# Attention scores over 64-key half-blocks in 32x64 tiles of TensorE, 76 score steps in place of 96

## The chip, the cores and the metric

The kernel runs on one core of a Trainium2 chip. The metric is the device time of one execution in microseconds. Five engines work side by side and meet through semaphores: TensorE (PE in the profile; its weight loads are PEld), VectorE (DVE), ScalarE (ACT), GpSimd (POOL) and SyncE (SP), which here only issues transfers. Each engine works off its own instructions in the order in which the program issues them.

## The reference

The input is normalized, and the sum of three terms is returned: the input itself, a sliding-window attention of 32 heads of 16 with a window of 256 keys, and a gated bilinear layer.

```python
xn = layernorm(x)                                  # x: 1 x 2048 x 512, bf16
# A: H = 32, Dh = 16, W = 256
q, k, v = split(xn @ wqkv)
scores = einsum("bhqd,bhkd->bhqk", q, k) * Dh ** -0.5
mask = (i - j >= 0) & (i - j < W)                  # query i, key j
o = einsum("bhqk,bhkd->bhqd", softmax(where(mask, scores, -1e9)), v)
a = o.reshape(B, S, D) @ wo
# B: F = 1792
b = ((xn @ w_gate) * (xn @ w_up)) @ w_down
return x + a + b
```

## The kernel before

The 2048 rows are cut into four chunks T of 512, and a chunk into four blocks of 128. All weights stay on the chip. The work falls into two kinds.

**Attention** goes by score steps. A group c has eight heads: four at even positions (parity 0) and four at odd positions (parity 1). The four heads e of one c and parity lie in four groups of 32 rows of TensorE, so their four matmuls run side by side, each in a 32x128 tile, and write four banks of the tile `S` (`scores`, L244). Keys stand on the partitions of the result and queries along the columns. A query block needs three key blocks: its own, masked to a triangle, the one before it, unmasked, and the one two before it, masked to the opposite triangle. `GROUPS` (L16) lays the twelve pairs of blocks of one chunk, c and parity into three strips of 512 columns: three steps, each with one exponential of 128x2048 on ScalarE (L252) and two or three triangles cut by GpSimd (L257, L261). With 4 chunks, 4 c, 2 parities and 3 strips there are 96 steps. `S` has one buffer, so a step's scores wait for the exponential of the step before.

Two steps (`LAG`) after the third strip of a c and parity, `values` (L277) multiplies the strips with V: four tiles of 128 rows x 32 columns side by side, one for each head, into the single accumulator `accb`. V has a column of ones, so the same matmul gives the sum of the softmax. VectorE transposes the accumulator (L284), takes the reciprocal (L286) and divides (L297); after parity 1 it transposes the result (L300).

**Fillers** are everything else: projections of the next chunk (`proj_v` L184, `proj_qk` L196), gate and up (L310, L321), down, the output projection and its store (L338, L344, L362), normalization of the next chunk. They are full 128x128 matmuls of 512 columns, four to a tile of gate or up. Their results go to a pool of three PSUM banks (`ps_m`): VectorE empties gate (L315), up (L325), K and Q (L201, L202, L207); ScalarE empties V (L188).

The order is written out in `run`: the loop goes over the score steps; after each it issues values that are due and then as many fillers as `upto` allows, which shares the planned TensorE time over the steps (here weighted by a step's blocks). The fillers' order is fixed in `fillers`: for each chunk down and output projection of the chunk before, then gate and up, then the projections of the next chunk. `before` and `after` keep a filler ahead of the step that needs it, or behind the one whose result it needs. Since engines work in order, what is issued on VectorE or ScalarE ahead of an eviction also runs ahead of it.

The start is separate: `setup` issues the first four blocks of x and the V weights alternately from SyncE and ScalarE (L62, L64), and `first_chunk` normalizes block by block, with the statistics of the fourth block on ScalarE and GpSimd (`norm_stats_act`, L133), and the first block's normalization and transposes in halves.

Of the kernel before, what the change touches and what calls it, by code (L numbers as in the profile page):

```python
# [11 lines left out]
ALU = mybir.AluOpType  # L12
# [3 lines left out]
GROUPS = (  # L16
    ((-2, 0, 0, 0), (0, 0, 2, 128)),
    ((-1, 0, 1, 0), (2, 2, 3, 256)),
    ((1, 1, 3, 0), (3, 3, 3, 384)),
)  # L20


class Kernel:
    def __init__(self, ctx, tc, x, wqkv, wo, wg, wu, wd, out):
        self.tc, self.nc = tc, tc.nc
        _, S, D = x.shape
        self.S, self.D, self.F = S, D, wg.shape[1]
        assert D == 512 and S % 512 == 0 and self.F % 256 == 0
        self.NT, self.NCH, self.NF = S // 128, S // 512, self.F // 128
        self.x_d, self.out_d = x.flatten_outer_dims(), out.flatten_outer_dims()  # L30
        self.w_d = dict(qkv=wqkv, o=wo, g=wg, u=wu, d=wd)

        def pool(name, bufs, **kw):
            return ctx.enter_context(tc.tile_pool(name=name, bufs=bufs, **kw))

        self.const = pool("const", 1)
        self.chunk2 = pool("chunk2", 2)
        self.chunk3 = pool("chunk3", 3)
        self.ppool = pool("ppool", 6)
        self.work = pool("work", 3)  # L40
        self.xpool = pool("xpool", 4)
        self.small = pool("small", 4)
        self.ypool = pool("ypool", 5)
        self.ps_s = pool("ps_s", 1, space=bass.MemoryType.PSUM)
        self.ps_a = pool("ps_a", 1, space=bass.MemoryType.PSUM)
        self.ps_m = pool("ps_m", 3, space=bass.MemoryType.PSUM)


    def setup(self):
# [11 lines left out]
        for b in range(4):  # L61
            (nc.scalar if b % 2 else nc.sync).dma_start(out=self.x[:, b, :], in_=xv[:, b, :])  # L62
        for k in (0, 2):
            (nc.scalar if k else nc.sync).dma_start(out=self.Wqkv[:, k:k + 2, 1024:1536], in_=wq[:, k:k + 2, 1024:1536])  # L64
        for lo in (512, 0):
# [32 lines left out]
        nc.gpsimd.memset(self.mhalf[:], -0.5)  # L98
        self.xnT, self.Q, self.hT, self.O, self.OT = {}, {}, {}, {}, {}
        self.K, self.Ko, self.V = {}, {}, {}  # L100
        self.strips, self.at = {}, {}

    def new_chunk(self, T):
# [5 lines left out]
        self.nc.gpsimd.memset(self.V[T][:, :, :, 16:18], 1.0)  # L109

# [22 lines left out]
    def norm_stats_act(self, t):  # L133

        nc = self.nc
        sums = self.small.tile([128, 2], F32, tag="sums", name="sums")
        for j, func in enumerate((ACT.Copy, ACT.Square)):
            junk = self.xpool.tile([128, 512], BF16, tag="xn", name="junk")
            nc.scalar.activation(out=junk[:], in_=self.x[:, t, :], func=func, accum_out=sums[:, j:j + 1])
        mv = self.small.tile([128, 1, 2], F32, tag="mv", name="mv")  # L140
        mean, sq = mv[:, 0, 0:1], self.small.tile([128, 2], F32, tag="sq", name="sq")
        nc.gpsimd.tensor_scalar(out=mean, in0=sums[:, 0:1], scalar1=1.0 / 512, scalar2=None, op0=ALU.mult)
        nc.gpsimd.tensor_scalar(out=sq[:, 0:1], in0=sums[:, 1:2], scalar1=1.0 / 512, scalar2=None, op0=ALU.mult)
        nc.gpsimd.tensor_tensor(out=sq[:, 1:2], in0=mean, in1=mean, op=ALU.mult)
        nc.gpsimd.tensor_tensor(out=mv[:, 0, 1:2], in0=sq[:, 0:1], in1=sq[:, 1:2], op=ALU.subtract)
        self.stats[t] = [mv, 0, None]

    def norm_apply(self, t):
# [3 lines left out]
        for c0, c1 in ((0, 256), (256, 512)) if t == 0 else ((0, 512),):  # L152
            nc.vector.tensor_scalar(out=xn[:, c0:c1], in0=self.x[:, t, c0:c1], scalar1=mv[:, j, 0:1],  # L153
                                    scalar2=rs[:, j:j + 1], op0=ALU.subtract, op1=ALU.mult)
        self.xns[t] = xn

    def norm_transpose(self, t, by_dma):
# [9 lines left out]
        for k0, k1 in ((0, 2), (2, 4)) if t == 0 else ((0, 4),):  # L167
            ps = self.ps_m.tile([128, 4, 128], BF16, tag="M", name="xTp")
            for k in range(k0, k1):
                nc.tensor.transpose(ps[:, k, :], xn[:, 128 * k:128 * k + 128], self.ident[:])  # L170
            nc.scalar.activation(out=self.xnT[T][:, b, k0:k1, :], in_=ps[:, k0:k1, :], func=ACT.Copy)
# [37 lines left out]
    def first_chunk(self):  # L209

        self.new_chunk(0)
        for b in (0, 1):
            self.norm_stats(b, 1)
            self.norm_scale(b, 1)
        self.norm_stats_act(3)
        self.norm_apply(0)
        self.norm_stats(2, 1)
        self.norm_scale(2, 1)
        self.norm_scale(3, 1)
        for b in (1, 2, 3):  # L220
            self.norm_apply(b)
        self.norm_transpose(0, False)
        for b in range(4):
            if b < 3:
                self.norm_transpose(b + 1, False)
            self.proj_v(b)
        self.proj_qk(0, 0, 1)
# [4 lines left out]
    def parts(self, T, i):  # L232
        return [p for p in GROUPS[i] if 4 * T + p[0] >= 0]

    def scores(self, T, c, par, i):

        nc = self.nc
        parts = self.parts(T, i)
        S = self.ps_s.tile([128, 4, 512], F32, tag="S", name="S")
        for kb, q0, q1, col in parts:  # L240
            n, (U, j) = 128 * (q1 - q0 + 1), divmod(4 * T + kb, 4)
            for e in range(4):
                rows = slice(32 * e, 32 * e + (32 if par else 16))
                nc.tensor.matmul(S[:, e, col:col + n],  # L244
                                 lhsT=(self.Ko if par else self.K)[U][rows, c, 128 * j:128 * j + 128],
                                 rhs=self.Q[T][rows, c, 128 * q0:128 * q0 + n],
                                 start=True, stop=True, tile_position=(32 * e, 0),
                                 skip_group_check=True)
        P = self.ppool.tile([128, 4, 512], BF16, tag="P", name="P")
        lo = parts[0][3]  # L250
        hi = parts[-1][3] + 128 * (parts[-1][2] - parts[-1][1] + 1)
        nc.scalar.activation(out=P[:, :, lo:hi], in_=S[:, :, lo:hi], func=ACT.Exp, scale=0.25)  # L252
        for kb, q0, q1, col in parts:
            for q in range(q0, q1 + 1):
                j = col + 128 * (q - q0)
                if q == kb:
                    nc.gpsimd.affine_select(out=P[:, :, j:j + 128], in_=P[:, :, j:j + 128],  # L257
                                            pattern=[[0, 4], [1, 128]], compare_op=ALU.is_ge,
                                            fill=0.0, base=0, channel_multiplier=-1)
                elif q == kb + 2:  # L260
                    nc.gpsimd.affine_select(out=P[:, :, j:j + 128], in_=P[:, :, j:j + 128],  # L261
                                            pattern=[[0, 4], [-1, 128]], compare_op=ALU.is_gt,
                                            fill=0.0, base=0, channel_multiplier=1)
        self.strips[(T, c, par, i)] = P

    def values(self, T, c, par):
# [4 lines left out]
        first = True  # L271
        for i in range(3):
            P = self.strips.pop((T, c, par, i))
            for kb, q0, q1, col in self.parts(T, i):
                n, (U, v) = 128 * (q1 - q0 + 1), divmod(4 * T + kb, 4)
                for e in range(4):
                    nc.tensor.matmul(acc[32 * e:32 * e + 17, 128 * q0:128 * q0 + n],  # L277
                                     lhsT=self.V[U][:, v, 8 * c + 2 * e + par, 0:17],
                                     rhs=P[:, e, col:col + n], start=first, stop=(i == 2),
                                     tile_position=(0, 32 * e), skip_group_check=True)  # L280
                first = False
# [84 lines left out]
    def fillers(self):  # L366
# [3 lines left out]
        NCH, NF, NG = self.NCH, self.NF, 24  # L370
# [11 lines left out]
        def project(T):  # L382
            add(0, lambda: self.new_chunk(T))
            for b in range(4):
                for ks in halves:
                    add(2, lambda t=4 * T + b, ks=ks: self.proj_v(t, ks), NG * T)
            for c in range(4):
                qk(T, c, NG * T + 6 * c)
# [25 lines left out]
        def wo(T, b, cs):  # L414
            add(len(cs), lambda: self.wo(T, b, cs), None, NG * T + 6 * cs[-1] + 5)

        qk(0, 1, 6, (0,))
        for c in range(2, 4):
            qk(0, c, 6 * c)
# [25 lines left out]
    def run(self):  # L445
        self.xns, self.stats, self.sums = {}, {}, {}
        self.setup()
        NCH, NG, LAG = self.NCH, 24, 2
        RESERVE = 38
        self.first_chunk()  # L450
        steps = [(T, c, par, i) for T in range(NCH) for c in range(4) for par in range(2) for i in range(3)]
        weight = [sum(p[2] - p[1] + 1 for p in self.parts(s[0], s[3])) + 1.7 for s in steps]
        SCORES, VALUES = 1.85, 3.5
        work = self.fillers()
        total = sum(w[0] for w in work) - RESERVE + SCORES * len(steps) + VALUES * (len(steps) // 3 - 1)
        done_w, spent, n = 0, 0, 0
# [15 lines left out]
        def values(g):  # L472
            nonlocal spent
            if g < 0 or steps[g][3] < 2:
                return False
            self.values(*steps[g][:3])
# [3 lines left out]
        def divide(g):  # L480
            nonlocal valued
            self.divide(*steps[g][:3])
            valued = g

        for g, s in enumerate(steps):
# [3 lines left out]
            done_w += weight[g]  # L489
            upto = total * done_w / sum(weight)  # L490
            if values(g - LAG):
                fill(min(spent + 4, upto), g)
                divide(g - LAG)
            fill(upto, g)
# [10 lines left out]
        self.wo(T, 3, (0, 1, 2, 3))  # L505
        self.store(T, 3, 0)
        self.store(T, 3, 1, True)
# [37 lines left out]
```

## Time and profile before

| | |
|---|---|
| runs | 280.48, 280.51, 282.27 us; median 280.51 |
| profiled execution | 280.48 us; span 278.7 us |
| TensorE busy | 271.6 us (97%), 2414 matmuls and as many weight loads |
| VectorE busy | 188.1 us (67%) |
| ScalarE busy | 184.5 us (66%), of it 170.0 in 96 exponentials |
| GpSimd busy | 164.4 us (59%), of it 156.4 in 240 triangle masks |
| matmuls of scores, of values | 704 (L244), 704 (L277) |

The span is the time between the first and the last instruction of one profiled execution; some 1.8 us lie around it. TensorE's matmuls are pipelined, so a sum of their durations is longer than the time in which they are started: a full matmul of 512 columns is shown with 380 ns, but four in a row take 0.86 us.

### The profile page before, as it was taken

The page shows a single profiled execution, that of the slowest core. Times are in us where ns is not written, and L with a number is a line of the kernel's source. Part 1 is how long each engine was busy: PE and PEld are TensorE (multiplying, and loading weights), DVE is VectorE, ACT ScalarE, POOL GpSimd, SP SyncE. Part 2 cuts the span into 40 slices and gives each one's busy share as a digit, 9 for nine tenths or more (in the row PEclk, how much of TensorE's full clock was granted, in tenths as well). Part 3 has the DMA queues.
Part 4 walks back from the last instruction along what each step waited for, and adds up shares of the span by engine and source line. Part 5 has one row for each costly group of instructions (what it writes and reads, how often), then busy time and mean ns, then how long its engine had stood idle before and what let it go on. Part 6 is the DMA issues. An engine that isn't in the chain of part 4 may idle for free.

```text
span 278.7 us, 5858 instructions
## 1 busy us (share of the span) xinstructions
PE 271.6 (97%) x2414; PEld 114.6 (41%) x2414; DVE 188.1 (67%) x337; ACT 184.5 (66%) x126; POOL 164.4 (59%) x288
## 2 busy tenths in 40 slices
PE   6999999999999999999999999999999999999994
PEld 5433333333434443434344344444343434434453
DVE  5277989879557778757946778774952467787222
ACT  4576666696667676778676767669675767666601
POOL 4226666755777665665867665666656565656420
PEclk9999999999999999999999999999999999999999
DMA  6999511000111100000012200000001000000002
GB/s 196 376 372 348 123 21 21 19 1 2 38 40 38 40 2 0 1 2 0 2 40 58 56 2 0 2 0 4 0 2 40 19 22 0 2 0 2 0 2 75
DMA packets 17194, 13.74 MB, mean 49 GB/s; under 512 B 7056, under 2 KB 17168, under 8 KB 17168
## 3 DMA queue, kind: packets, MB, share of 16 engines
q1 hardware_dynamic: 16320, 12.65, 14.8%
q10 hardware_dynamic: 848, 0.72, 0.8%
q8 instruction: 19, 0.31, 0.4%
q14 instruction: 7, 0.06, 0.1%
HBM read 9.70 MB, written 2.10 MB: 42 GB/s over the span
## 4 chain that ended last, share of the span: by engine, by line
PE 86%; ACT 6%; DVE 3%; DMA 2%; POOL 1%; issue 1%; ACTq 0%; DVEq 0%
PE psd L338 18%; PE up L321 17%; PE gp L310 17%; PE S L244 10%; PE qkp L196 9%; PE accb L277 7%; PE psd L344 5%; ACT P L252 4%; PE vp L184 3%; ACT V L188 1%; DMA x<-in_A_x_dram 1%; DVE st L118 1%; DMA out_dram<-y 1%; DVE gsb L315 1%; DVE xn L153 1%
## 5 line engine op out<-in xcount | busy, mean ns | idle before, releaser
L252 ACT ACTIVATE P<-S 128x2048 bf16<-128x2048 f32 (+2 forms) x96 | 170.0, 1771 | 74.3 <-PE S L244 62.6
L257 POOL TENSOR_SCALAR_AFFINE_SELECT P<-P 128x512 bf16<-128x512 bf16 x128 | 84.5, 660 | 54.8 <-ACT P L252 54.7
L261 POOL TENSOR_SCALAR_AFFINE_SELECT P<-P 128x512 bf16<-128x512 bf16 x112 | 71.9, 642 | 38.6 <-ACT P L252 38.6
L321 PE MATMUL up<-xnT,Wu 128*128 128x512 bf16 x224 | 60.0, 380 | 0.1
L310 PE MATMUL gp<-xnT,Wg 128*128 128x512 bf16 x224 | 59.7, 380 | 0.0
L338 PE MATMUL psd<-Wd,hT 128*128 128x512 bf16 (+1 forms) x238 | 54.3, 367 | 0.0
L284 DVE STREAM_TRANSPOSE at<-accb 128x512 f32<-128x512 f32 x32 | 22.8, 713 | 39.0 <-PE accb L277 39.0
L325 DVE TENSOR_TENSOR hT<-up,gsb 128x512 bf16<-128x512 f32 x56 | 38.1, 681 | 7.8 <-PE up L321 5.8
L315 DVE CAST gsb<-gp 128x512 bf16<-128x512 f32 x56 | 37.9, 677 | 5.9 <-PE gp L310 5.8
L338 PEld LDWEIGHTS <-hT 128*128 128x128 bf16 x238 | 21.5, 98 | 24.9 <-issue 4.7
L310 PEld LDWEIGHTS <-Wg 128*128 128x128 bf16 x224 | 20.0, 98 | 26.1 <-issue 5.2
L196 PE MATMUL qkp<-xnT,Wqkv 128*128 128x512 bf16 x128 | 30.5, 380 | 0.0
L321 PEld LDWEIGHTS <-Wu 128*128 128x128 bf16 x224 | 19.6, 97 | 26.4 <-issue 7.1
L277 PE MATMUL accb<-P,V 128*17 128x384 bf16 (+2 forms) x704 | 25.4, 276 | 0.0
L362 DVE TENSOR_TENSOR y<-psd,x 128x512 bf16<-128x512 f32 (+1 forms) x15 | 9.9, 666 | 17.0 <-PE psd L344 17.0
L244 PE MATMUL S<-Q,Ko 32*128 32x256 bf16 (+2 forms) x352 | 18.4, 275 | 0.5 <-ACT P L252 0.2
L297 DVE TENSOR_TENSOR on<-at,rz 128x256 bf16<-128x256 f32 x32 | 18.6, 580 | 0.4
L244 PE MATMUL S<-Q,K 16*128 16x256 bf16 (+2 forms) x352 | 18.4, 276 | 0.1
L196 PEld LDWEIGHTS <-Wqkv 128*128 128x128 bf16 x128 | 11.4, 98 | 14.6 <-issue 2.7
L277 PEld LDWEIGHTS <-V 128*17 128x17 bf16 x704 | 13.8, 90 | 8.7 <-issue 5.3
L201 DVE CAST K<-qkp 128x512 bf16<-128x512 f32 x16 | 11.0, 689 | 9.2 <-PE qkp L196 8.9
L344 PE MATMUL psd<-Wo,OT 128*128 128x512 bf16 (+1 forms) x68 | 16.8, 367 | 0.0
(45 smaller groups left out, 142.9 us busy)
## 6 DMA issues: line engine op xcount, KB each, us to landing
Wg<-in_B_w_gate_dram SPq DMA_DIRECT2D x2, 896.0 KB, 10.4
Wu<-in_B_w_up_dram SPq DMA_DIRECT2D x2, 896.0 KB, 12.4
Wd<-in_B_w_down_dram SPq DMA_DIRECT2D x1, 1792.0 KB, 15.8
out_dram<-y SPq DMA_DIRECT2D x14, 128.0 KB, 1.7
Wqkv<-in_A_wqkv_dram SPq DMA_DIRECT2D x2, 512.0 KB, 7.4
x<-in_A_x_dram SPq DMA_DIRECT2D x1, 1024.0 KB, 10.3
x<-in_A_x_dram SPq DMA_DIRECT2D x1, 512.0 KB, 11.1
Wo<-in_A_wo_dram SPq DMA_DIRECT2D x1, 512.0 KB, 15.6
```

Of the source, the lines that this page charges most:

```text
L196: nc.tensor.matmul(ps[:], lhsT=self.Wqkv[:, k, lo:lo + 128], rhs=self.xnT[T][:, :, k, :], start=(k == 0), stop=(k == 3))
L244: nc.tensor.matmul(S[:, e, col:col + n], lhsT=(self.Ko if par else self.K)[U][rows, c, 128 * j:128 * j + 128], rhs=self.Q[T][rows, c, 128 ...
L252: nc.scalar.activation(out=P[:, :, lo:hi], in_=S[:, :, lo:hi], func=ACT.Exp, scale=0.25)
L257: nc.gpsimd.affine_select(out=P[:, :, j:j + 128], in_=P[:, :, j:j + 128], pattern=[[0, 4], [1, 128]], compare_op=ALU.is_ge, fill=0.0, base ...
L261: nc.gpsimd.affine_select(out=P[:, :, j:j + 128], in_=P[:, :, j:j + 128], pattern=[[0, 4], [-1, 128]], compare_op=ALU.is_gt, fill=0.0, bas ...
L277: nc.tensor.matmul(acc[32 * e:32 * e + 17, 128 * q0:128 * q0 + n], lhsT=self.V[U][:, v, 8 * c + 2 * e + par, 0:17], rhs=P[:, e, col:col + ...
L310: nc.tensor.matmul(ps[:], lhsT=self.Wg[:, k, 128 * f:128 * f + 128], rhs=self.xnT[T][:, :, k, :], start=(k == 0), stop=(k == 3))
L315: nc.vector.tensor_copy(out=self.gsb[:], in_=ps[:])
L321: nc.tensor.matmul(ps[:], lhsT=self.Wu[:, k, 128 * f:128 * f + 128], rhs=self.xnT[T][:, :, k, :], start=(k == 0), stop=(k == 3))
L325: nc.vector.tensor_tensor(out=self.hT[T][:, f, :], in0=ps[:], in1=self.gsb[:], op=ALU.mult)
L338: nc.tensor.matmul(ps, lhsT=self.hT[T][:, f, 128 * b:128 * b + 128], rhs=self.Wd[:, f, c0:c1], start=(f == 0), stop=False)
L344: self.nc.tensor.matmul(ps, lhsT=self.OT[T][:, c, 128 * b:128 * b + 128], rhs=self.Wo[:, c, c0:c1], start=False, stop=(c == 3))
```

## The change

**Half-blocks.** The key block is cut into two halves of 64 keys. A half-block's scores use a tile of 32 rows x 64 columns of TensorE, half 0 into partitions 0 to 63 and half 1 into partitions 64 to 127 of the same bank; with four heads and two halves there are eight such tiles. In the same column of a strip both halves have the same query. A 64-key half-block needs only the queries from its own 64-block to the fourth after it, so a window takes five half-blocks of 64 in place of three blocks of 128.

**Strips.** A strip of kind `EVEN` or `ODD` holds, for key blocks J-2, J and J+2 (J is 0 or 1), all pieces of both halves: six pieces of 64, 128, 320, 320, 128 and 64 queries, for four heads each. What is left over, two unmasked pairs of blocks for each parity, goes for both parities into one strip `PLAIN` in the former 32x128 tiles. A chunk and c thus have five steps in place of six; the first chunk, with no keys before it, has four, seven pieces each. That makes 76. Every exponential is of 128x2048.

**Masks.** Columns 64 to 127 and 384 to 447 hold two half-triangles each and are cut on VectorE by a minimum with a constant tile `diag` (0 or 2^126), one instruction for both and all four heads. The other two to each side, 64 wide on all partitions, are cut by GpSimd: four instructions of 128x256 per strip, three in the first chunk.

**Values.** Where both halves of a strip belong to the same key block, V is used as before. Where only one half does, V is needed with zeros in the other half: tiles `Vu`, `Vl0`, `Vl1`, set to zero once (`zero_halves`) and filled for each chunk by two copies of 64 partitions x 2304 elements (`copy_halves`, VectorE). A strip becomes seven value pieces (six in the first chunk), a plain strip two per parity, four heads each.

**Around it.** The planned time is shared equally over the steps. The start loses its special forms: x comes in three transfers and the V weights in one, all from SyncE; the fourth block's statistics are taken on VectorE, and the first block is neither normalized nor transposed in halves. The pool `work` has two buffers in place of three and `ypool` four in place of five. The last two stores change places.

```diff
-GROUPS = (
-    ((-2, 0, 0, 0), (0, 0, 2, 128)),
-    ((-1, 0, 1, 0), (2, 2, 3, 256)),
-    ((1, 1, 3, 0), (3, 3, 3, 384)),
-)
+EVEN, ODD, PLAIN = 0, 1, 2
+BIG = 2.0 ** 126
...
-        for b in range(4):
-            (nc.scalar if b % 2 else nc.sync).dma_start(out=self.x[:, b, :], in_=xv[:, b, :])
-        for k in (0, 2):
-            (nc.scalar if k else nc.sync).dma_start(out=self.Wqkv[:, k:k + 2, 1024:1536], in_=wq[:, k:k + 2, 1024:1536])
-        for lo in (512, 0):
+        for lo, hi in ((0, 1), (1, 2), (2, 4)):
+            nc.sync.dma_start(out=self.x[:, lo:hi, :], in_=xv[:, lo:hi, :])
+        for lo in (1024, 512, 0):
             nc.sync.dma_start(out=self.Wqkv[:, :, lo:lo + 512], in_=wq[:, :, lo:lo + 512])
...
+    def zero_halves(self, j):
+        for h in (0, 1) if j == 0 else (1,):
+            self.nc.gpsimd.memset(self.Vh[j][h][64 - 64 * h:128 - 64 * h], 0.0)
+
+    def copy_halves(self, T):
+        for h in range(2):
+            rows = slice(64 * h, 64 * h + 64)
+            self.nc.vector.tensor_copy(out=self.Vh[T % 2][h][rows], in_=self.V[T][rows])
...
+    def batches(self, T):
+        if T == 0:
+            return [(EVEN, 0), (ODD, 0), (EVEN, 1), (ODD, 1)]
+        return [(EVEN, 0), (ODD, 0), (PLAIN, None), (EVEN, 1), (ODD, 1)]
+
+    def score_pieces(self, T, kind, par):
+        if kind == PLAIN:
+            return [(p, kb, h, q, 128, 256 * p + col)
+                    for p in range(2) for kb, q, col in ((-1, 0, 0), (2, 384, 128)) for h in (None,)]
+        J, q = kind, 128 * kind
+        if T == 0:
+            first = [(par, 2, 0, 384 + 64 * J, 64, 0), (par, 2, 1, 384 + 64 * J, 64, 0)]
+            second = [(par, J, 1, q + 64, 64, 64)]
+        else:
+            first = [(par, J - 2, 0, q, 64, 0), (par, J - 2, 1, q, 128, 0)]
+            second = []
+        return first + second + [
+            (par, J, 0, q, 320, 64), (par, J, 1, q + 64, 320, 128),
+            (par, J + 2, 0, q + 256, 128, 384), (par, J + 2, 1, q + 320, 64, 448)]
...
+            if h is not None:
+                keys, outs = slice(128 * j + 64 * h, 128 * j + 64 * h + 64), slice(64 * h, 64 * h + 64)
             for e in range(4):
...
+                nc.tensor.matmul(S[outs, e, col:col + n],
+                                 lhsT=(self.Ko if p else self.K)[U][rows, c, keys],
+                                 rhs=self.Q[T][rows, c, q:q + n],
+                                 start=True, stop=True, tile_position=(32 * e, outs.start),
                                  skip_group_check=True)
...
+        nc.vector.tensor_tensor(out=both, in0=both, in1=m.unsqueeze(1).to_broadcast([128, 4, 2, 64]),
+                                op=ALU.min)
...
+    def value_pieces(self, T, kind, par):
+        if kind == PLAIN:
+            return [(256 * par, 2, -1, 0, 128), (256 * par + 128, 2, 2, 384, 128)]
+        J, q = kind, 128 * kind
+        if T == 0:
+            first = [(0, 2, 2, 384 + 64 * J, 64)]
+        else:
+            first = [(0, 2, J - 2, q, 64), (64, 1, J - 2, q + 64, 64)]
+        return first + [(64, 0, J, q, 64), (128, 2, J, q + 64, 256), (384, 1, J, q + 320, 64),
+                        (384, 0, J + 2, q + 256, 64), (448, 2, J + 2, q + 320, 64)]
...
-            upto = total * done_w / sum(weight)
+            upto = total * (g + 1) / len(steps)
...
+                T, c, par = due[g - LAG]
+                if (c, par) == (3, 1):
+                    self.copy_halves(T + 1)
```

## Prediction

> **What bounds the kernel now.** I read the page's busy times and chain first, then the chain in order of time and the timeline for one stretch of the third chunk, then the busy time by stage, the waits, and the groups of VectorE.
>
> ```profile
> span 278.7 us, 5858 instructions
> ...
> PE 271.6 (97%) x2414; PEld 114.6 (41%) x2414; DVE 188.1 (67%) x337; ACT 184.5 (66%) x126; POOL 164.4 (59%) x288
> ...
> PE 86%; ACT 6%; DVE 3%; DMA 2%; POOL 1%; issue 1%; ACTq 0%; DVEq 0%
> ```
>
> TensorE sets the end: busy 97%, and 86% of the chain. The clock row is full speed throughout. So first I ask what the change does to TensorE's own sequence. The chain in order of time shows what a score step and a values step cost there:
>
> ```profile
> 157.44 0.33 PE S L244 x8
> 157.77 0.97 PE up L321 x4
> 158.74 0.86 PE gp L310 x4
> ...
> 160.80 0.76 PE accb L277 x24
> 161.56 0.97 PE gp L310 x4
> ```
>
> Four full matmuls of 512 columns take 0.86 us, 0.216 each. Four concurrent row tiles stream 512 columns for all four heads in the same 0.216, so the 0.33 of a score step holds 0.11 of turning over, and the 0.97 in place of 0.86 behind it another 0.11: a step costs 0.44, of which 0.22 is there once per step whatever it holds. Values of 1536 columns: 0.76, where streaming alone is 0.65.
>
> **TensorE, part by part.** (a) Steps fall from 96 to 76: 20 x 0.22 = **-4.4 us**. (b) Columns streamed by scores: before 24 x 1536 + 8 x 1152 (first chunk) = 46,080; after 76 x 512 = 38,912, if the two 64-key halves run side by side. 7,168 columns at 0.216/512 = **-3.0**. (c) Values stream the same columns as before: a strip of seven pieces has 640, two strips and 256 of the plain one make 1536; in the first chunk 2 x 576 = 1152. But they come in more pieces. Matmuls of scores go from 704 to 1792 (112 per chunk and c), of values from 704 to 1920 (24 per c and parity to 64, 48 in the first chunk), all matmuls from 2414 to 4718. In the records a quad of 256 or 384 columns starts 109 or 163 ns after the one before, 2 to 3 ns over its streaming; ten more quads in a values step and some four more in a score step, at 3 ns each, are about 1.7, and I add a little for the loads of the 64-column weights, a shape the trace does not have: **+2.0** (ends: 0, and 0.22 per strip or 14 in all if the halves do not overlap, as a third rival).
>
> **Can the pieces be issued that fast?** A values step and the score step before it are now 24 + 64 = 88 load-matmul pairs, against this densest stretch of today:
>
> ```profile
> 160.40 0.40 PE L244 MATMUL S<-Q,Ko 32*128 32x256 bf16 x8
> 160.73 0.83 PE L277 MATMUL accb<-P,V 128*17 128x128 bf16 x24
> 161.50 1.04 PE L310 MATMUL gp<-xnT,Wg 128*128 128x512 bf16 x4
> ```
>
> Here 32 pairs start in 1.10 us, and the same 32 are the most that the trace shows close together; over 128 pairs the densest it has is 96 ns a pair. So at least 32 can stand ready, and nothing shows how fast the next ones come. One place is near: at 7.69 us TensorE resumes behind a wait of its own sequencer (for the V weights), with nothing queued.
>
> ```profile
> 7.69 0.56 PEld L184 LDWEIGHTS <-xnT 128*128 128x128 bf16 x4 [0.26 <-issue]
> 7.72 1.02 PE L184 MATMUL vp<-Wqkv,xnT 128*128 128x512 bf16 x4
> ...
> 8.66 0.23 PEld L170 LDWEIGHTS <-xn 128*128 128x128 bf16 x4 [0.40 <-DVE xn L153]
> 8.66 0.40 PE L170 MATMUL xTp<-ident,xn 128*128 128x128 bf16 x4
> ```
>
> The first matmul follows its load by 31 ns and the next load comes 2 ns on, where the queued pair at 8.66 needs 4 ns: 33 ns for two instructions. At 33 ns a pair beyond the first 32: 56 x 0.033 = 1.85 us, where the streaming needs 1.2; 0.65 lost in 24 values steps and (40 x 0.033 - 1.05) = 0.27 in the 8 of the first chunk, 17.8 us. Lower end 0 (quads leave at about 3 ns an instruction). Were none ready ahead, 88 pairs would take 3.0 us for 1.2 and 72 (first chunk) 2.4 for 1.05: 54. I take **+4**: nearer the lower end, since the slow place is single and both its instructions carried a wait.
>
> [...]
>
> **VectorE.** The change moves one of the three mask shapes from POOL to VectorE: 64 instructions on 512 elements, behind the exponential of the same step. It adds eight copies of 64 rows x 2304.
>
> ```profile
> L257 POOL TENSOR_SCALAR_AFFINE_SELECT P<-P 128x512 bf16<-128x512 bf16 x128 | 84.5, 660 | 54.8 <-ACT P L252 54.7
> ...
> L325 DVE TENSOR_TENSOR hT<-up,gsb 128x512 bf16<-128x512 f32 x56 | 38.1, 681 | 7.8 <-PE up L321 5.8
> ...
> L297 DVE TENSOR_TENSOR on<-at,rz 128x256 bf16<-128x256 f32 x32 | 18.6, 580 | 0.4
> ...
> L202 DVE TENSOR_SCALAR Ko<-K,odd 128x512 bf16<-128x512 bf16 x16 | 7.0, 440 | 0.6
> ```
>
> The minimum lies between 440 (512 bf16, one tensor) and 681 (two tensors, one in PSUM); I take 0.55: 35 us. A copy of 2304 elements is priced between 0.44 (as if 512) and 3.1 (4.5 x 681); I take 1.2, 10 us. VectorE goes from 188 to about 233. Whether that matters is read by stage:
>
> ```profile
> 20.00:36.00 16.00, 15.95 (x125) 6.34 (x124) 14.10 (x27) 10.80 (x8) 10.20 (x18) 1.00 0.76 226
> ...
> 89.00:122.00 33.00, 32.96 (x314) 13.48 (x306) 25.50 (x43) 22.52 (x12) 19.87 (x33) 1.00 0.04 10
> ```
>
> The third busy time of a line is VectorE's. In a gate/up stage every 0.86 us of TensorE leaves a bank that VectorE must empty (0.68), and it is at 77 to 88% already. Some 9 steps per stage, 7 with a minimum, make 26 into 30 of 32. The load would just fit; the order does not. Today POOL waits for exponentials (54.8 us ahead of one mask alone) and nobody cares. Now VectorE waits: from the start of a score step to the end of its exponential it is 2.4 us (S at 160.40, ACT 160.93 + 1.88), and queued behind the minimum are the evictions of all gate and up tiles issued after that step, the accumulator's transpose and the division. TensorE has three banks, 2.6 us of work. In a step without values, 0.44 + 3 x 0.86 = 3.0 us pass before a fourth tile needs a bank; VectorE gives the first one back at 2.45 + 0.55 + 0.68 = 3.7, and the next score step fills 0.44 of that gap. In a step with values, 0.71 + 0.25 (transpose, reciprocal) come ahead of that eviction and 0.58 (division) of a later one: banks come about 0.7 us late. Some 15 of the 32 values steps fall into the four gate/up stages: **+10** (ends: 0 if VectorE works off enough ahead of each minimum, 20 if each of 38 steps there loses 0.5). In the down stages nothing is lost: a bank is filled for 3.9 us there.
>
> **POOL, ACT.** POOL's 240 masks are half as wide: at the slope from the 128-element select (0.29 us) to 0.66 about 0.41, 100 us in place of 156; the three memsets of 2304 (2.4 us each by the rows of 128 and 256) fall into its idle time from 9 to 16 us, or delay masks by less than the two steps between scores and values. ACT runs 76 exponentials of 1.88, 143 for 170 us. Neither sets the end: worth **0**.
>
> **First blocks.** One queue issues all of x and the V weights, which are awaited at 7.6 us; their issue (1.72 now) moves behind three x transfers by some 0.5 us. The bytes ahead are the same; the fourth block's statistics return from ACT to VectorE, where they end by about 8.05 and the apply by 9.4, as today (9.48). **+0.5** (0 to 1.5). The order of the last two stores is on different engines: 0.
>
> **Sum**, against the profiled execution's own 280.48 us (span 278.7, 1.8 around it; the median of the runs is 280.51): 280.5 - 4.4 - 3.0 + 2.0 + 4 + 10 + 0.5 = **289.6 us**, 3% slower.
>
> **Rivals.** (1) TensorE's saving arrives whole: no issue limit, VectorE keeps up, halves overlap: 280.5 - 7.4 + 2.0 + 0.5 = 275.6, or 274 without the extra for loads. For it: VectorE's load fits each stage, TensorE today loses almost nothing to other engines. Against it: the order on VectorE. It decides if banks come late by less than 0.15 us per values step. (2) Issue is the bound: from 33 ns a pair upwards. 275.6 + 17.8 = 293 at that row, 330 if none stood ready; VectorE's stall is then hidden in it. About 310. (3) The two 64-column halves of one row group do not run together, the change's step not doing what it says: 64 strips x 0.216 = +14, with half of VectorE's stall hidden: 275.6 + 14 + 5 = 295.
>
> **How the numbers follow.** Forecast (282 to 298) 0.48; (1) 0.24, a little of it reaching over 277.7; (2) 0.18; (3) 0.10. The range 274 to 316 leaves out the lower edge of (1) and the upper half of (2). A measurement of this kernel tells about 1% from no change (277.7 to 283.3): most of (1) is faster, its upper edge and the lower edge of the forecast are the same, the rest slower: 0.23, 0.12, 0.65. The likeliest case alone runs from 282 to 298.
>
> **What would show it.** Right: in gate/up stages TensorE waits for VectorE's evictions, VectorE's wait for the exponential stands ahead of the minimum, and the score step without values still costs about 0.44. Issue: values steps longer than 0.8 us with loads late by no one's release. Halves apart: score steps of 0.55 and more. The forecast fails if TensorE stays at 97% with no waits on VectorE.

## The result, and the profile after

The changed kernel takes 317.5 us (median of four runs, 316.7 to 319.2) against 280.5 before: a ratio of 1.131 [1.125, 1.138], 37 us slower. The forecast had 289.6 and a range that ended at 316. The direction is as forecast; the size is four times as large.

The page of after, first busy times, the rows of TensorE and of its granted clock over the span, and the shares of the chain that ended last. The profiled execution took 319.23 us.

```profile
span 317.1 us, 10496 instructions
...
PE 279.7 (88%) x4718; PEld 130.0 (41%) x4718; DVE 210.0 (66%) x410; ACT 156.6 (49%) x101; POOL 130.9 (41%) x291
...
PE   7778988796969979989898999889889998989995
...
PEclk9989999998968999999999999999999999999998
...
PE 48%; DVE 26%; ACT 21%; issue 2%; POOL 2%; DMA 1%; ACTq 0%
```

No engine is near its limit: TensorE stood at 97% and now idles for 37 us, and the chain runs through VectorE and ScalarE for 47% of the span. A chain that leaves the busiest engine for others that are themselves idle a third or half of the time is a sign of waits, not of work. Ahead of the last slice the granted clock is lower in three places.

The groups of after that answer to those shown of before; after the bar busy time, mean ns of one, and the engine's idle time before them with its releaser:

```profile
L281 POOL TENSOR_SCALAR_AFFINE_SELECT P<-P 128x256 bf16<-128x256 bf16 x112 | 57.3, 530 | 149.4 <-ACT P L269 149.4
...
L278 DVE TENSOR_TENSOR P<-P,diag 128x512 bf16<-128x512 bf16 x64 | 27.9, 436 | 83.4 <-ACT P L269 83.4
...
L362 DVE TENSOR_TENSOR hT<-up,gsb 128x512 bf16<-128x512 f32 x56 | 38.0, 679 | 3.1
...
L334 DVE TENSOR_TENSOR on<-at,rz 128x256 bf16<-128x256 f32 x32 | 13.5, 421 | 0.3
```

The minimum works for 27.9 us, but VectorE stands idle for 83.4 us ahead of it, waiting for the exponential. Whether that idle time costs anything shows in who waits for VectorE. The waits of TensorE in after (waited for; us in total, times, longest):

```profile
PE up L358 <- DVE gsb L352: 9.7, 15, 1.4
PE gp L347 <- DVE hT L362: 6.6, 11, 0.9
PE qkp L195 <- DVE Q L206: 4.7, 3, 2.5
PE psd L381 <- DVE OT L337: 3.8, 2, 2.8
```

None of these four stands among TensorE's waits of before. The chain in order of time shows one whole cycle; first two score steps without loss, then one with:

```profile
187.25 0.36 PE S L263 x24
187.61 0.97 PE up L358 x4
188.57 0.86 PE gp L347 x4
189.44 0.86 PE up L358 x4
190.30 0.36 PE S L263 x24
190.66 0.79 PE accb L315 x64
191.45 0.97 PE gp L347 x4
...
193.71 0.42 PE S L263 x24
...
194.21 1.89 ACT P L269
...
196.12 0.43 DVE P L278
196.54 0.61 DVE gsb L352
...
197.20 0.59 PE up L358 x2
197.79 0.42 PE S L263 x24
```

What TensorE did in that last step besides, from its timeline (start, us, then in brackets idle time and releaser):

```profile
194.00 0.61 PE L347 MATMUL gp<-xnT,Wg 128*128 128x512 bf16 x2
194.65 1.02 PE L358 MATMUL up<-xnT,Wu 128*128 128x512 bf16 x4
195.57 1.02 PE L347 MATMUL gp<-xnT,Wg 128*128 128x512 bf16 x4
197.20 0.59 PE L358 MATMUL up<-xnT,Wu 128*128 128x512 bf16 x2 [0.60 <-DVE gsb L352]
```

The step at 187.25 holds three whole tiles, up, gate and up: three banks, and nothing is lost. The step at 193.71 also holds three tiles' worth, but cut otherwise: the second half of a gate tile, an up tile, a gate tile, and then the first half of an up tile, for which there was no bank. All that time VectorE stood in front of a minimum whose exponential ended at 196.09, with the evictions queued behind it. The step took 4.08 us (193.71 to 197.79). Undisturbed it is 0.36 + 0.11 + 12 x 0.216 = 3.06, so 1.0 us is lost, 0.77 of it at the bank and the rest in short hitches about it.

The same stretch on the timeline of VectorE (start, us, then in brackets idle time and releaser):

```profile
196.12 0.43 DVE L278 TENSOR_TENSOR P<-P,diag 128x512 bf16<-128x512 bf16 x1 [0.60 <-ACT P L269]
196.46 0.68 DVE L352 CAST gsb<-gp 128x512 bf16<-128x512 f32 x1
...
200.19 0.43 DVE L278 TENSOR_TENSOR P<-P,diag 128x512 bf16<-128x512 bf16 x1 [1.65 <-ACT P L269]
200.53 0.71 DVE L321 STREAM_TRANSPOSE at<-accb 128x512 f32<-128x512 f32 x1
201.28 0.25 DVE L323 RECIPROCAL rz<-at 128x16 f32<-128x16 f32 x1
201.45 0.63 DVE L362 TENSOR_TENSOR hT<-up,gsb 128x512 bf16<-128x512 f32 x1
201.99 0.41 DVE L334 TENSOR_TENSOR on<-at,rz 128x256 bf16<-128x256 f32 x1
202.44 0.71 DVE L337 STREAM_TRANSPOSE OT<-on 128x512 bf16<-128x512 bf16 x1
203.08 0.65 DVE L352 CAST gsb<-gp 128x512 bf16<-128x512 f32 x1
```

The gate tile evicted at 196.46 is the one whose last matmul was issued before 194.6. VectorE idles 1.65 us ahead of the second minimum and then has all its work at once. That minimum stands in the step with values that began at 197.72; behind it come the transpose and the reciprocal, then an eviction, then the division and a second transpose, then the next eviction. TensorE pays for both only in the step after, which began at 201.13. It is a plain step, without a minimum of its own:

```profile
202.13 1.02 PE L347 MATMUL gp<-xnT,Wg 128*128 128x512 bf16 x4 [0.59 <-DVE hT L362]
203.78 1.02 PE L358 MATMUL up<-xnT,Wu 128*128 128x512 bf16 x4 [0.63 <-DVE gsb L352]
```

**Counting it over the trace.** For each step I took the time from its first score matmul to the next step's, less the undisturbed time of the same matmuls as above. This gives 45.7 us lost in after and 0.2 before. (The count is some 2.8 us too high: with 4.5 saved on TensorE, below, and 0.5 at the start it makes 322.0 for the 319.2 measured.) By stage: gate and up 22.3, projections 14.2, down 9.2. Within gate and up, 22 steps **without** values lose 21.8 us, 0.99 each, and 17 steps **with** values lose 0.5 in all. The steps without values hold 3.14 tiles on average, those with values 2.32. The fillers' pool has three banks.

The step that loses is not always the one whose minimum is to blame. For each loss in these 22 steps one can go back on VectorE, from the eviction that TensorE waited for to the last wait for an exponential ahead of it. Seven steps (6.7 us) wait behind their own minimum. Nine (10.8 us) wait behind the minimum of the step with values ahead of them and that step's transpose and reciprocal, some behind its division too; four of these nine are plain steps. Another four (3.9 us) wait behind both, and two lose next to nothing.

**The clock.** Busy times by stretch, for three stretches of after in which the clock was halved (PE, PEld, DVE, ACT, POOL, then the clock, DMA share and GB/s):

```profile
21.80:25.25 3.45, 3.45 (x9) 1.05 (x7) 2.89 (x6) 0.00 (x0) 0.06 (x1) 0.51 1.10 348
76.40:79.90 3.50, 3.50 (x82) 1.56 (x79) 2.45 (x5) 0.74 (x1) 0.00 (x0) 0.51 0.02 5
90.10:96.90 6.80, 6.13 (x29) 2.13 (x30) 3.80 (x7) 1.88 (x1) 0.93 (x3) 0.50 0.15 39
```

In 13.75 us TensorE is busy 13.1 at half speed, work of some 6.5 at full speed: **about 6 us** more, a part of the 45.7 counted above. (The profiled execution was the slowest of the four; its mean clock was 0.976, that of the others 0.981 to 0.986.) All three lie in steps that the count puts down to the projections and the down stages. Each spell follows a stretch at full clock (1.00) in which TensorE was busy for little of the time: 1.49 of the 3.40 us from 18.40, 1.35 of the 3.90 from 72.50, 1.22 of the 3.40 from 86.70. A wait on VectorE of 1.9 to 2.8 us lies in it or reaches over its end. None of the three stretches was wholly idle, and what brings the clock down was not run apart.

### The profile page after: what moved, and what is told of

Same layout as the page of the kernel before. It is cut to its first block, busy times and chain, and to the rows that moved or that the text cites. A ratio compares the mean times of both kernels' runs of the same rounds, so it can differ in the third digit from the quotient of the medians.

```text
span 317.1 us, 10496 instructions
## 1 busy us (share of the span) xinstructions
PE 279.7 (88%) x4718; PEld 130.0 (41%) x4718; DVE 210.0 (66%) x410; ACT 156.6 (49%) x101; POOL 130.9 (41%) x291
## 4 chain that ended last, share of the span: by engine, by line
PE 48%; DVE 26%; ACT 21%; issue 2%; POOL 2%; DMA 1%; ACTq 0%
ACT P L269 21%; PE psd L375 16%; PE S L263 7%; PE up L358 6%; PE gp L347 6%; DVE at L321 4%; DVE P L278 4%; PE psd L381 4%; PE qkp L195 4%; DVE gsb L352 3%; PE accb L315 3%; DVE hT L362 3%; DVE OT L337 2%; PE vp L183 2%; DVE on L334 2%
## 5 line engine op out<-in xcount | busy, mean ns | idle before, releaser
L269 ACT ACTIVATE P<-S 128x2048 bf16<-128x2048 f32 x76 | 142.6, 1877 | 136.5 <-PE S L263 100.1
L281 POOL TENSOR_SCALAR_AFFINE_SELECT P<-P 128x256 bf16<-128x256 bf16 x112 | 57.3, 530 | 149.4 <-ACT P L269 149.4
L278 DVE TENSOR_TENSOR P<-P,diag 128x512 bf16<-128x512 bf16 x64 | 27.9, 436 | 83.4 <-ACT P L269 83.4
L285 POOL TENSOR_SCALAR_AFFINE_SELECT P<-P 128x256 bf16<-128x256 bf16 x128 | 54.5, 447 | 0.0
L195 PE MATMUL qkp<-xnT,Wqkv 128*128 128x512 bf16 x128 | 32.7, 392 | 6.9 <-DVE Q L206 4.7
L315 PE MATMUL accb<-P,V 128*17 128x64 bf16 (+2 forms) x960 | 26.5, 222 | 0.0
L315 PE MATMUL accb<-P,Vu 128*17 128x64 bf16 x512 | 21.0, 194 | 0.0
L315 PEld LDWEIGHTS <-V 128*17 128x17 bf16 x960 | 17.3, 92 | 5.1 <-issue 0.7
L315 PE MATMUL accb<-P,Vl 128*17 128x64 bf16 x448 | 19.1, 194 | 0.0
L263 PE MATMUL S<-Q,Ko 32*64 32x64 bf16 (+3 forms) x896 | 17.5, 239 | 0.0
L263 PE MATMUL S<-Q,K 16*64 16x64 bf16 (+3 forms) x896 | 17.3, 237 | 0.0
```

Source lines behind the costliest of these rows:

```text
L195: nc.tensor.matmul(ps[:], lhsT=self.Wqkv[:, k, lo:lo + 128], rhs=self.xnT[T][:, :, k, :], start=(k == 0), stop=(k == 3))
L263: nc.tensor.matmul(S[outs, e, col:col + n], lhsT=(self.Ko if p else self.K)[U][rows, c, keys], rhs=self.Q[T][rows, c, q:q + n], start=True ...
L269: nc.scalar.activation(out=P[:], in_=S[:], func=ACT.Exp, scale=0.25)
L278: nc.vector.tensor_tensor(out=both, in0=both, in1=m.unsqueeze(1).to_broadcast([128, 4, 2, 64]), op=ALU.min)
L281: nc.gpsimd.affine_select(out=P[:, :, col:col + 64], in_=P[:, :, col:col + 64], pattern=[[0, 4], [-1, 64]], compare_op=ALU.is_gt, fill=0.0 ...
L285: nc.gpsimd.affine_select(out=P[:, :, col:col + 64], in_=P[:, :, col:col + 64], pattern=[[0, 4], [1, 64]], compare_op=ALU.is_ge, fill=0.0, ...
```

## The experiments

Three theories stood at the start. **A, order**: the minimum waits for its exponential, and evictions queue behind it. **B, load**: VectorE has more work, wherever it stands. **C**: the parts around the change (pools, shares, start, zeroing).

**1. The same minimum, issued later.** Each minimum is held back to just ahead of the next step's scores, when its exponential is mostly done.

```diff
-        nc.vector.tensor_tensor(out=both, ...)
+        self.late = lambda: nc.vector.tensor_tensor(out=both, ...)
...
             fill(-1, g)
+            if self.late:
+                self.late()
...
             self.scores(*s)
```

> The changed kernel with one thing different: the minimum of a score step is issued on VectorE behind the fillers of that step, just ahead of the next step's scores, and not right behind the exponential. VectorE does exactly the same work. Theory A (order: the minimum waits some 2.4 us for the exponential and the evictions of gate, up, K and Q queue behind it): TensorE loses almost nothing, 277 to 283 us, the idle time ahead of the minimum falls from 83 us to under 15, and the clock stays full. Theory B (load: 28 us of minimum and 6 us of copies more than VectorE can hide): still 310 to 318. Theory C (something else in the change: smaller pools, equal shares, the start): also 310 or more.

Measured 279.7 us, 0.996 of before [0.994, 0.998]. Its page and the group of the minimum:

```profile
span 277.8 us, 10496 instructions
...
PE 266.7 (96%) x4718; PEld 128.0 (46%) x4718; DVE 213.7 (77%) x410; ACT 156.4 (56%) x101; POOL 125.0 (45%) x291
...
L278 DVE TENSOR_TENSOR P<-P,diag 128x512 bf16<-128x512 bf16 x64 | 29.1, 455 | 6.2 <-ACT P L269 6.1
```

Instructions and their work are the same (VectorE is busy 3.7 us longer than in after), and 38 us are gone. Step by step, after takes 39.6 us longer than this run, for 39.3 measured between the two profiled executions. VectorE's wait falls from 83.4 to 6.2 us, and the clock stays full (0.999 in the profiled execution, 0.976 in that of after). B and C are out for nearly all of the loss.

**2. A minimum that waits for nothing, in its old place.** It works on constant scratch tiles, so the half-triangles stay uncut.

```diff
-        nc.vector.tensor_tensor(out=both, in0=both, in1=m..., op=ALU.min)
+        nc.vector.tensor_tensor(out=self.scr2[:], in0=self.scr1[:], in1=m..., op=ALU.min)
```

> The changed kernel with the minimum in its old place on VectorE, but reading and writing constant scratch tiles, so that it waits for no exponential; the half-triangles that it cut are left uncut. Same instructions, same order, the wait alone gone. Theory A: 277 to 284. Theory B: 310 to 318, as the load is the same. Theory C: 310 or more.

```profile
L280 DVE TENSOR_TENSOR scr<-scr,diag 128x512 bf16<-128x512 bf16 x64 | 28.8, 450 | 0.1
```

Measured 279.7 us (one run). Place, number and length of the instruction are as in after; only what it waits for is gone, and with it the loss. Neither its work nor its place costs anything without the wait. (The values no longer wait for the minimum here either, but in after TensorE shows no wait of values for it.)

**3. The minimum put into the kernel before**, 64 of them in place of masks of GpSimd (strips 0 and 2), without half-blocks.

```diff
-                if q == kb:
+                if q == kb and i != 1 and kb in (0, 1):
+                    nc.vector.tensor_tensor(out=P[:, :, j:j + 128], in0=P[:, :, j:j + 128], in1=..., op=ALU.min)
+                elif q == kb:
```

> The kernel before, with one part of the change alone: in the first and third strip of each c and parity, the own-block triangle of 128x512 is cut by a minimum on VectorE right behind the exponential in place of GpSimd, 64 in all. Scores, values, start and pools stay as they were. Theory A: 305 to 325 us, the loss of the change without its half-blocks. Theory B: VectorE's load of 188 + 28 us, without the copies: 295 to 310. Theory C: within 3 us of 280.5.

Measured 296.8 us, 1.056 [1.052, 1.061]: 16.4 us for 64 minima, 0.26 each. Its waits:

```profile
DVE P L261 <- ACT P L256: 52.4, 53, 2.8
...
PE up L329 <- DVE gsb L323: 4.1, 8, 0.8
PE gp L318 <- DVE hT L333: 2.6, 5, 0.8
```

The same waits as in after, at full clock (1.00). It is below what A expected and in B's range, so by its length it would speak for load; runs 1 and 2 exclude that in the changed kernel, and a late minimum was not run in this one. But why does the same wait cost 0.26 us here and 0.59 (38 / 64) there? Three things differ. Here a step in gate and up without values holds 2.56 tiles, in after 3.14; by the count of the trace, steps here lose 0.51 with 3 tiles and 0.29 to 0.36 with 2 or 2.5. No step with values but the last holds a minimum here, while in after all of them do. And the clock fell in after.

**4. One in every step**, 96 minima in the kernel before (the condition becomes `(i, kb) != (2, 3)`).

> The kernel before with the own-block triangle on VectorE in all three strips of each c and parity, 96 minima in place of 64 (which cost 16.4 us). If the loss goes by the number of minima, that is 24.5 us: 302 to 308. If it falls on single steps (those without values in gate/up and projection stages, where strip two stands as well) much the same, 300 to 312. If the loss of the changed kernel (37.8 us for 64) came from the share of steps that hold a minimum, 4 of 5 and not 2 of 3, then at 3 of 3 it must be above 315.

Measured 307.7 us, 1.096 [1.093, 1.099]: 27.2 us, 0.28 each. The loss goes roughly with the number of minima, and the share of steps that hold one does not explain the 0.59 of after. Of the 32 minima added to run 3 all but one stand in steps with values; they cost 10.8 us, 0.34 each in place of 0.26.

**5. Tiles moved from one kind of step to the other**, in the changed kernel with the minimum in its early place. If banks decide, the loss follows the tiles.

```diff
+        share = [19.5 if g - LAG in due else 12.8 for g in range(len(steps))]
...
-            upto = total * (g + 1) / len(steps)
+            upto = total * sum(share[:g + 1]) / sum(share)
```

> The changed kernel with its early minimum and the planned time shared out unequally: steps in which values fall get 19.5 parts, the others 12.8. In gate/up stages the steps without values now hold 3 to 3.5 tiles of fillers and lose some 1.0 us each, those with values 2 to 2.5 and lose nothing; with the shift it should be about 2.5 and 3. Theory A1 (what counts is how many tiles want a bank behind a score step, three being there): the steps without values lose 0.3 to 0.6 each, as in the kernel before with minima, those with values up to 0.7; 300 to 313 us in all. If the loss is one wait per minimum whatever the tiles: 315 to 320, and 1.0 per step without values as before.

Measured 309.6 us, 1.104 [1.101, 1.108]. In gate and up, by the same count of the traces:

| | tiles per step | lost per step |
|---|---|---|
| after, steps without values (22) | 3.14 | 0.99 us |
| after, steps with values (17) | 2.32 | 0.03 |
| shifted, steps without values (23) | 2.50 | 0.24 |
| shifted, steps with values (17) | 3.22 | 0.93 |

The loss went over to the other kind of step with the tiles. So the tiles behind a waiting minimum decide: at 2.5 tiles, hardly any step of the later chunks loses by its own minimum; at three and more, begun ones counted, a fourth bank is wanted too early. The work of a step with values does count as well. In the shifted kernel nearly all waits of gate and up stand behind the minimum, the transpose and the reciprocal of such a step. How much these two add to the minimum's own wait is read from the traces and was not run apart.

**6. The minimum behind the first filler tile**, a place between early and late: in the loop, `fill(min(spent + 4, upto), g)` and `self.late()` come after the values and ahead of the division.

> The changed kernel with the minimum issued behind the first tile (four matmuls) of the step's fillers: half way between its old place (317.5 us) and the late one (279.7). Theory A1, banks (TensorE has three banks, and stands still only when the eviction of the first tile behind a score step comes after the fourth tile wants its bank): the first tile is now evicted about 2.0 us after the start of the step, the fourth wants it at 3.0, so nearly all of the loss is gone, 279 to 285, although VectorE still idles for the exponential. Theory A2, idle time (the loss follows the time that VectorE idles ahead of the minimum, 83 us in the changed kernel, then about half): 293 to 303.

Measured 287.6 us, 1.025 [1.022, 1.027], between the two versions of A. VectorE still waits 21.3 us ahead of the minimum, in 23 places. Gate and up of the later chunks lose 0.10 us in a step without values; step by step against run 1, 2.5 us of what is left lie in the first chunk, where VectorE also normalizes, 2.4 in three steps about one stretch of 3.4 us at half clock (mean of the execution 0.994), and 3.1 in single steps of the later chunks. Why these keep that much was not taken further.

**7. The mask on GpSimd**, as a product with a tile of 0 and 1 (`BIG = 1.0`, `nc.gpsimd.tensor_tensor`, `ALU.mult`).

> The changed kernel with the mask taken off VectorE: the same place in the program, but one GpSimd multiplication by a tile of 0 and 1. VectorE has neither the wait nor the 28 us. Theory A and B: both 277 to 283, and if A holds alone, no faster than with the late minimum by more than 2 us. Theory C: 310 or more. Against all: if GpSimd's multiplication is slow (over 1.2 us each), values wait for masks and it ends above 285.

Measured 284.7 us, 1.013 [1.009, 1.017], above what was expected. The group of the mask, and of VectorE's division here and in run 1:

```profile
L278 POOL TENSOR_TENSOR P<-P,diag 128x512 bf16<-128x512 bf16 x64 | 74.5, 1164 | 70.6 <-ACT P L269 70.4
...
L334 DVE TENSOR_TENSOR on<-at,rz 128x256 bf16<-128x256 f32 x32 | 27.2, 850 | 0.3
```

```profile
L334 DVE TENSOR_TENSOR on<-at,rz 128x256 bf16<-128x256 f32 x32 | 15.0, 468 | 0.3
```

GpSimd now does the waiting, 70.6 us of it, and TensorE shows no wait for a mask. But with its products of 1.16 us VectorE's division takes 850 ns in place of 468, and `Ko` 734 in place of 447. The 23 divisions that overlap a product take 984 ns on average, the other nine 393 to 620: taking work off VectorE slowed what stayed.

**8. The parts around it, in the kernel before**: transfers and normalization at the start, pools and the order of the last stores as in the changed kernel.

```diff
-        self.work = pool("work", 3)
+        self.work = pool("work", 2)
...
+        for lo, hi in ((0, 1), (1, 2), (2, 4)):
+            nc.sync.dma_start(out=self.x[:, lo:hi, :], in_=xv[:, lo:hi, :])
```

> The kernel before with what stands around the half-blocks in the change, without the padded V: the start of the changed kernel, the pools of two and four buffers, the exchanged last stores. Theory A: all of that together costs 0 to 1.5 us, 280.5 to 282. Theory C (these parts matter): above 283.

Measured 279.9 us, 0.998 [0.997, 0.999]. These parts cost nothing by themselves. The equal shares and the zeroing are not in this run; both stand in run 1, at 279.7 us.

**9. Late minimum with the start of before, and zeroing in four pieces per tile** (run 1, plus the former start, plus `for v in range(4)` around the memset).

> The late minimum with the start of the kernel before (x and V weights from two queues, statistics of the fourth block on ScalarE and GpSimd, first block in halves), and GpSimd's zeroing of the padded V in four pieces each. In the changed kernel one apply of normalization took 2.19 us in place of 0.41 while GpSimd zeroed 64x2304. Theory A with a sum of the steps (20 steps fewer save 3.9 us on TensorE, the start is worth 0.5 to 1.5 and the zeroing up to 1.8): 276.5 to 278.5, the shortest so far. If the start is worth nothing: 279.7.

Measured 278.7 us, 0.994 [0.992, 0.996], just above what was expected: 1 us better than run 1. The first scores start at 14.76 us in place of 15.44, and from there to the last step the two runs take the same time within 0.1 us. What the former start and what the zeroing gives was not run apart. In the changed kernel the zeroing delayed a normalization; timeline of VectorE, then of GpSimd, in after:

```profile
7.07 0.41 DVE L153 TENSOR_SCALAR xn<-x,mv,rs 128x512 bf16<-128x512 bf16 x1
8.25 2.19 DVE L153 TENSOR_SCALAR xn<-x,mv,rs 128x512 bf16<-128x512 bf16 x1 [0.77 <-POOL rs L145]
```

```profile
8.27 2.01 POOL L119 MEMSET Vu<- 64x2304 bf16 x1
```

The same instruction takes 0.41 us alone and 2.19 beside the memset: its record starts 0.02 us ahead of the memset's and ends 0.16 us after it. Why the two end so close together, no run shows.

**10. The V copies on ScalarE**, on top of run 9 (`nc.scalar.activation(..., func=ACT.Copy)`).

> As e6_start, and the eight copies of V into the padded tiles go to ScalarE (about 2 us each by GpSimd's rate, 0.8 on VectorE). VectorE is relieved by 6 us, of which 1.6 stand in the first gate/up stage, where the late minimum still leaves TensorE waiting some 4 us: 275.5 to 278 if that stage is bound by VectorE's load; 278 to 281 if the copies delay the first exponentials or the V evictions on ScalarE.

Measured 291.0 us, 1.036 [1.034, 1.039]. The copies, and TensorE's first wait:

```profile
L128 ACT ACTIVATE Vl<-V 64x2304 bf16<-64x2304 bf16 x4 | 8.5, 2120 | 0.0
```

```profile
PE S L286 <- ACT P L292: 7.2, 4, 2.2
```

Two copies of 2.12 us (0.78 on VectorE) stand ahead of an exponential, four times; the exponential holds the only buffer of `S`, and the next scores wait for it. The clock fell again, to 0.94 on average from 130 to 160 us and to 0.97 from 190 to 250; by the mean of 0.988 over the execution, that is some 7 us at half clock. It is the error of the change itself, made on another engine.

**11. The normalization of the second chunk on GpSimd**, on top of run 9 (`nc.gpsimd if 4 <= t < 8`), since in run 9 VectorE is busy for 15.54 of the 16 us from 24 to 40.

> As e6_start (late minimum, start of the kernel before: 278.7 us), with the four applies of the normalization of the second chunk, which fall into the first gate/up stage, on GpSimd in place of VectorE. VectorE is busy 15.5 of 16 us there (24 to 40 us) and TensorE loses some 2.4 us in its steps without values. If load is what holds that stage now: 276 to 278. If not, or if GpSimd's apply slows VectorE's own instructions: 278.5 to 280.

Measured 278.1 us, 0.991 [0.988, 0.993], faster than both kernels, and between the two forecasts (276 to 278 and 278.5 to 280). Each of the four takes 2.10 us on GpSimd, and steps in gate and up of the first chunk lose 1.5 us in place of 2.4. That is in keeping with load as a part of what holds this stage.

## Why the prediction had the direction right and the size wrong

**Steps and columns (a, b, c): right, somewhat too high.** Score steps are 0.36 us (0.33 before), values 0.79 (0.76). By starts of matmuls, scores and values together take 51.0 us of TensorE in run 1 and 53.5 before, and 20 fewer changes of tile form save some 0.1 each (0.97 in place of 0.86 us for the tile behind a score step): about 4.5 saved for 5.4 forecast. The two halves run side by side, which settles rival 3. Of the 4.5 run 1 shows 0.8 and run 11 2.4: run 1 starts its first scores 0.8 us later, and by the count of the trace (some 2.8 us too high) it still loses some 6 us to waits of TensorE where the kernel before loses 0.2, a part of it in the first chunk, where VectorE is full (busy 90% or more in each slice of the page from 20.8 to 48.6 us). What remains of it was not taken apart.

**Issue (+4): wrong, it is 0.** The chain shows 24 + 64 = 88 load and matmul pairs in 0.36 + 0.79 = 1.15 us, 13 ns a pair. The 33 ns that the forecast read at one slow place, and rival 2 with it, do not hold. (The forecast also counted 72 pairs for a step of the first chunk; with seven score pieces it is 76.)

**The minimum's and the copies' length: too high.** 0.436 us for 0.55, 0.78 for 1.2. Load was overpriced.

**The start (+0.5): right for the first scores.** The first scores start at 15.13 us for 14.66. But the zeroing on GpSimd, priced at nothing because it would fall into idle time, is idle time of the wrong engine: it held up VectorE for 1.8 us.

**VectorE's stall (+10): this step failed.** The mechanism was named, the waits are those forecast (gate and up wait for VectorE, VectorE for the exponential), and rival 1, in which the saving arrives whole, falls with it. The term should have been about 38: 317.5 less the 279.7 of run 1. What it priced came close: it gave 15 steps with values in gate and up 0.7 us each for the minimum, transpose, reciprocal and division, and by the count such work costs 10.8 us, though in nine steps, over 1 us each, and one step later; that the two sums agree is partly luck. The larger part was put at nothing:
- Steps without values were to lose nothing, since "the next score step fills 0.44 of that gap". But shares are equal by planned time, so such a step holds 3.14 tiles on average, and it often starts in the middle of one. A fourth bank is wanted before the next score step comes. Seven of them lose 6.7 us behind their own minimum, four more lose 3.9 behind both. Reading TensorE's chain for how many tiles a step holds would have shown 2.56 before, and the equal shares over 76 steps in place of 96 make it more.
- It counted gate and up only. The projections had no term. There VectorE empties K and Q, and TensorE waits for up to 2.5 us at once. Of the down stages the forecast said that "nothing is lost: a bank is filled for 3.9 us there". That looks at the bank, but the output projection also waits for `OT`, which stands behind the minimum, too (3.8 us in two waits). By the count these stages lost 23.4 of 45.7 us.
- A wait was taken to cost its own length. In three spells the clock also fell, to 0.50 or 0.51, behind waits of 1.9 to 2.8 us: some 6 us, worked out from the stretches above. All of it lies in the projections and the down stages, so of the 23 us there some 17 are left for waits.

The upper end given for this term, 20 (0.5 for each of 38 steps), comes close to what gate and up lost by the count (22.3). What no bound of the term held were the other stages and the clock. That the measured 317.5 lies near the upper end of the range, 316, is luck: that end was drawn for a limit of issue, and there was none.

## What to carry to other kernels

Before moving an instruction to an engine that works in order, ask what it waits for and what stands behind it: 0.44 us of work placed 2 us too early cost 0.59 us each, and the same instruction issued just ahead of the next step cost next to nothing. Count how much the consumers can run on meanwhile, here three banks against the tiles of a step, in every stage and not only in the one with the most work. Look for the loss in the step behind, too: the work that piles up behind a wait is paid for when the banks run out. A late issue of the waiting instruction is the first remedy; moving work to another engine, as runs 7 and 10 show, brings the waits or the slower instruction along: a product of 1.16 us on GpSimd for a minimum of 0.44, a copy of 2.12 us on ScalarE for one of 0.78.

## What the runs showed of the hardware

- A score step and a values step, 24 load and matmul pairs in 32x64 tiles and 64 in 128x32 tiles, in pieces of 64 to 320 columns, left at 13 ns a pair over the 88 pairs of after's chain (0.36 + 0.79 us), without a sign of an issue limit.
- In after the clock was halved (0.50 and 0.51) in three spells. Each stood behind a stretch of 3.4 to 3.9 us in which TensorE was busy for 1.2 to 1.5 us, 35 to 44% of the time.
- VectorE's instructions took longer beside instructions of GpSimd with which they share no data: in after a normalization 2.19 us beside a memset of 2.01, 0.41 alone; in run 7, with products of 1.16 us on GpSimd, a division 850 ns on average, 468 in run 1.
